# Attention and low-rank mixer: V in four row groups of the array, tails by a block-diagonal V, U into one group per head pair

## Chip, cores, metric

One core of one Trainium2 chip. The metric is the device time of a launch in microseconds (us), median of the runs.

## The reference, cut to what matters

Eight batches of causal attention with a decay bias (8 heads, 576 tokens, 64 per head), whose output x (576 x 512 per batch) goes through a low-rank mixing over tokens (rank 32) and a feed-forward:

```python
xt = x.transpose(0, 2, 1)                    # 512 x 576 per batch
h  = xt @ U @ V                              # U 576 x 32, V 32 x 576
u  = x + h.transpose(0, 2, 1)
out = u + np.maximum(u @ w_ch1, 0.0) @ w_ch2  # 512 -> 2048 -> 512
```

The change concerns `xt @ U @ V`. A "head pair" is 128 rows of xt; a batch has four.

## The kernel before

TensorE's order is written out by hand as tokens: SEQ for batches 0 and 1, PAIR for every later head pair. `U` is mix_in, `u` its copy out of PSUM, `Y` is mix_out (V), `y` adds x^T and writes u^T, `x` turns x by DMA, `F` is one step of feed-forward (four 512-column matmuls), `A`/`a` attention times v and its division, `D`/`E` scores, `G` the transposes of q and k on VectorE, `L` a step of the set-up of the decays, `p` a filler matmul (on the tile `warm`, its result unused). The other letters do not matter here.

```python
def mix_in(b):                       # U
    zp = z.rearrange("p (n c) -> p n c", n=PB)          # PB = 4 pairs
    for t in range(4):               # token block t into 32 PSUM rows, all four pairs at once
        nc.tensor.matmul(zp[ds(t * R, R)], lhsT=U_sb[:, t, :], rhs=x_of[b][:, :, t, :], start=True, stop=False, ...)
    for i in range(PB):              # the last 64 tokens of pair i
        nc.tensor.matmul(zp[ds(i * R, R), i, :], lhsT=U_sb[:, 4, :], rhs=x_of[b][:, i, 4, :], start=False, stop=True, ...)

def mix_out(n):                      # V, one pair; V_sb holds four stacked copies of V, so K = 128 sums the four partial products
    ...                              # cut: the 576 tokens in two pieces, two pairs share a bank `rest`
    if not mixed:                    # batches 0 and 1: x^T of the tail by an identity matmul
        nc.tensor.matmul(rest, lhsT=x_part(n, 4), rhs=identity[:, :64], start=True, stop=False, ...)
    for dst, lo, hi in pieces:
        nc.tensor.matmul(dst, lhsT=z_of[b][:, hp], rhs=V_sb[:, lo:hi], start=mixed, stop=True, ...)

xT = [stage[...] for i in range(3)]  # ring for x^T of batches 2 to 7
```

## Time and profile before

| | before |
|---|---|
| time, median of 4 runs | 370.0 us (369.4 to 370.3) |
| span of the profiled run | 367.9 us |
| TensorE, VectorE, ScalarE busy | 97%, 51%, 57% |
| U per batch, V per batch, in TensorE's stream | 0.48 us, 0.98 us |
| from one batch's U to the next, steady stage | 38.26 us |

The busy share says which engine is the bound; what an operation costs is read from the start times of matmuls, since each is still "busy" while the next already streams (a 512-column matmul is listed with 379 ns, the next one starts after 216). "Slot" below means this 0.216 us, and "stop" a gap beyond the slot. How to read the lines: in a timeline, start and duration in us, engine, line of the kernel, operation, tile written <- tiles read, shapes, count, and in brackets the idle time before with what ended it; in a list of waits, total us, times, longest. The lines follow inside the prediction.

### The profile page before, as it was taken

How to read it: one execution, taken by the hardware profiler on the slowest of the kernel's cores; microseconds unless marked ns; L12 is line 12 of the kernel's file. 1: busy time of each engine (PE TensorE's matmuls, PEld its weight loads, DVE VectorE, ACT ScalarE, POOL GpSimd, SP SyncE). 2: the span in 40 equal slices, each digit the busy share in tenths (PEclk: the TensorE clock that was granted, in tenths of full speed). 3: DMA queues.
4: the chain of work that ended last, by engine and by line, in shares of the span. 5: the costliest groups of instructions: out<-in, count | busy, mean ns of one | idle time of the engine just before them, and what ended most of it. 6: DMA issues, size and time to landing. Idle time of an engine off the chain costs nothing.

```text
span 367.9 us, 7782 instructions
## 1 busy us (share of the span) xinstructions
PE 355.9 (97%) x3036; PEld 197.1 (54%) x3036; DVE 187.5 (51%) x404; ACT 209.0 (57%) x407; POOL 108.6 (30%) x177
## 2 busy tenths in 40 slices
PE   8797999799999999999999999999999999999995
PEld 4576656356656655555555555555555444444443
DVE  7878756656658942864286536654453133011011
ACT  7697996248955686348734873388337602602600
POOL 8747461766435418040904080000000000000000
PEclk9999999999999999999999999999999999999999
DMA  7999999999999999995998899545115122113112
GB/s 95 165 185 124 143 152 205 169 241 188 154 152 174 186 155 149 157 161 109 150 136 144 148 114 119 152 114 77 51 64 98 37 76 85 30 43 99 31 41 74
DMA packets 112156, 45.53 MB, mean 124 GB/s; under 512 B 96448, under 2 KB 104000, under 8 KB 112120
## 3 DMA queue, kind: packets, MB, share of 16 engines
q0 software_dynamic: 65760, 18.54, 63.1%
q1 hardware_dynamic: 46360, 26.49, 36.9%
q8 instruction: 24, 0.39, 0.5%
q14 instruction: 12, 0.10, 0.1%
HBM read 37.73 MB, written 10.03 MB: 130 GB/s over the span
## 4 chain that ended last, share of the span: by engine, by line
PE 88%; DMA 5%; POOL 3%; DVE 2%; issue 1%; ACT 0%; POOLq 0%; ACTq 0%
PE pwork L477 34%; PE pwork L497 33%; PE pscore L265 10%; PE pwork L344 7%; DMA v_slot<-in_v_dram 3%; DMA U_sb<-in_moe_U_dram 2%; PE pwork L440 2%; POOL hT L120 1%; POOL v_slot L146 1%; PE pwork L375 1%; DVE turned L250 1%; DVE uT L463 0%; DVE x_sb L360 0%; DVE o_sb L510 0%; POOL stage L127 0%
## 5 line engine op out<-in xcount | busy, mean ns | idle before, releaser
L330 ACT ACTIVATE pT<-pscore 128x512 bf16<-128x512 f32 (+1 forms) x224 | 112.5, 568 | 69.6 <-PE pscore L265 67.2
L477 PE MATMUL pwork<-uT,w_sb 128*128 128x512 bf16 x576 | 134.1, 379 | 0.0
L497 PE MATMUL pwork<-w_sb,hT 128*128 128x512 bf16 (+2 forms) x592 | 132.0, 373 | 0.6 <-DVE o_sb L510 0.6
L484 ACT ACTIVATE hT<-pwork 128x512 bf16<-128x512 f32 x144 | 86.4, 618 | 53.9 <-PE pwork L477 53.3
L497 PEld LDWEIGHTS <-hT 128*128 128x128 bf16 x592 | 55.9, 98 | 60.2 <-issue 1.1
L477 PEld LDWEIGHTS <-w_sb 128*128 128x128 bf16 x576 | 53.9, 98 | 57.3 <-issue 1.5
L265 PE MATMUL pscore<-slot 128*128 128x128 bf16 (+4 forms) x576 | 61.9, 240 | 2.6 <-DVE slot L236 1.3
L250 DVE STREAM_TRANSPOSE turned<-qk_sd 128x576 bf16<-128x576 bf16 x48 | 54.2, 1130 | 7.6 <-DMA qk_sd<-in_q_dram 7.2
L510 DVE TENSOR_TENSOR o_sb<-pwork,stage 128x512 f32<-128x512 f32 (+2 forms) x37 | 24.8, 671 | 57.8 <-PE pwork L497 57.7
L265 PEld LDWEIGHTS <-slot 128*128 128x128 bf16 x576 | 39.7, 98 | 23.2 <-DVE slot L236 1.4
L359 DVE RECIPROCAL rec<-pwork 128x5 f32<-128x5 f32 x64 | 12.1, 188 | 77.0 <-PE pwork L344 76.7
L138 POOL DMA_DIRECT2D qk_sd<-in_q_dram x48 | 27.2, 578 | 77.6 <-DVE pT L333 38.3
L344 PEld LDWEIGHTS <-pT 128*128 128x128 bf16 x960 | 35.2, 98 | 7.1 <-issue 0.3
L344 PE MATMUL pwork<-v_slot,pT 128*128 128x65 bf16 x960 | 38.6, 194 | 0.2 <-DVE slot L236 0.2
L138 POOL DMA_DIRECT2D qk_sd<-in_k_dram x48 | 27.1, 575 | 22.2 <-DMA w_sb<-in_moe_w_ch_dram 15.5
L360 DVE TENSOR_TENSOR x_sb<-pwork,rec 128x320 bf16<-128x320 f32 x64 | 31.5, 492 | 2.2
L333 DVE TENSOR_TENSOR pT<-pT,keep 128x512 bf16<-128x512 bf16 (+1 forms) x84 | 28.1, 342 | 8.1 <-ACT pT L330 7.8
L146 POOL DMA_DIRECT2D v_slot<-in_v_dram x32 | 28.3, 907 | 3.5 <-DMA w_sb<-in_moe_w_ch_dram 2.4
L461 DVE TENSOR_TENSOR uT<-pwork,stage 128x384 bf16<-128x384 f32 (+7 forms) x48 | 19.1, 450 | 16.3 <-PE pwork L440 16.3
L236 DVE COPY slot<-pwork 64x576 bf16<-64x576 bf16 x21 | 16.7, 798 | 4.3 <-PE pwork L224 3.3
L557 PE MATMUL pwork<-warm 128*128 128x512 bf16 x38 | 10.7, 431 | 1.3 <-DVE warm L116 1.3
L440 PE MATMUL pwork<-V_sb,z_sb 128*128 128x512 bf16 (+6 forms) x64 | 11.7, 286 | 0.0
(76 smaller groups left out, 112.9 us busy)
## 6 DMA issues: line engine op xcount, KB each, us to landing
out_dram<-o_sb SPq DMA_DIRECT2D x35, 256.0 KB, 4.8
slot<-turned SPq DMA_DIRECT2D x96, 72.0 KB, 4.2
v_slot<-in_v_dram POOLq DMA_DIRECT2D x32, 128.0 KB, 7.3
w_sb<-in_moe_w_ch_dram POOLq DMA_DIRECT2D x8, 512.0 KB, 10.8
qk_sd<-in_q_dram POOLq DMA_DIRECT2D x48, 72.0 KB, 4.7
qk_sd<-in_k_dram POOLq DMA_DIRECT2D x48, 72.0 KB, 5.6
stage<-in_q_dram POOLq DMA_DIRECT2D x2, 288.0 KB, 9.4
stage<-in_k_dram POOLq DMA_DIRECT2D x2, 288.0 KB, 10.0
```

The source lines that it names most:

```text
L138: nc.gpsimd.dma_start(out=qk_t[g][ds(32 * a, 32), c, :].rearrange("p (n f) -> p n f", n=6), in_=src[g // 2, 4 * (g % 2) + a].rearrange("(n ...
L146: nc.gpsimd.dma_start(out=vt[:, t, :, 0:D], in_=v[b, :, ds(t * 128, 128), :].rearrange("h p d -> p h d"),)
L250: nc.vector.transpose(turned[:, e, c].rearrange("p (n m t) -> p n t m", n=6, t=3), src[:, c].rearrange("p (n t e d) -> p e n t d", n=6, t= ...
L265: nc.tensor.matmul(dst, lhsT=head_of(h)[:, ds(S + j * 128, 128)], rhs=head_of(h)[:, lo:hi], start=start, stop=stop and not bias, skip_grou ...
L330: nc.scalar.activation(dst, src, EXP, scale=scale)
L333: nc.vector.tensor_tensor(p, p, m, op=ALU.min)
L344: nc.tensor.matmul(po[:, i, :], lhsT=p_of(h)[:, ds(spot(j, i), 128)], rhs=v_slots[h // H % 3][:, j, h % H, :], start=(j == 0), stop=(j == ...
L360: nc.vector.tensor_tensor(x_of[b][:, h % H // 2, :, ts(h % 2, D)], po[:, :, 0:D], rec.to_broadcast([128, 5, D]), op=ALU.mult,)
L477: nc.tensor.matmul(f1, lhsT=w1_sb[nf // 4][:, kt, ds(nf % 4 * 128, 128)], rhs=uT[:, g % 4, kt, :], start=(kt == 0), stop=(kt == 3),)
L484: pending.append(lambda nf=nf, f1=f1: nc.scalar.activation(hT[:, nf, :], f1, RELU))
L497: nc.tensor.matmul(f2[:, lo:hi], lhsT=hT[:, nf, ds(i * 128, 128)], rhs=w2_sb[nf // 4][:, nf % 4, lo:hi], start=(nf == 0), stop=nf == NF - ...
L510: nc.vector.tensor_tensor(o_sb[:, lo:hi].rearrange("p (d c) -> p d c", c=128), f2[:, lo:hi].rearrange("p (d c) -> p d c", c=128), u_sb[g % ...
```

## The change

Intent: V has only 32 rows, so four pairs can use four 32-row strips of the array at once. For that U must leave pair i's product in partitions 32i to 32i+31, and four PSUM banks must be open together. The tails (64 tokens) of all pairs come from one matmul with a block-diagonal V. The whole token order, the order of loads and the bank list were redone around it, and x^T got a fourth buffer because all four pairs of a batch are now alive together.

```diff
 def mix_in(b):
-        for t in range(4): ... four 512-column, then four 128-column matmuls
+        for t in range(5):
+            for i in range(PB):
+                nc.tensor.matmul(
+                    z[ds(i * R, R), 0:128],
+                    lhsT=U_sb[:, t, :],
+                    rhs=x_of[b][:, i, t, :],
+                    start=(t == 0), stop=(t == 4), ...)
 def mix_keep(copy, b):
-        copy(z.rearrange("p n c -> p (n c)"), z_of[b])      # 512 columns
+        copy(z, z_of[b][:, 0:128])
-    def mix_out(n): ...
+    def mix_out(b):
+        for i, n in enumerate(pairs):
+            nc.tensor.matmul(
+                mix_of[n],                                  # four banks
+                lhsT=z_of[b][ds(i * R, R), :],
+                rhs=V_sb[ds(i * R, R), 0:512],
+                start=mixed, stop=True, ...)
+        rest = pwork()
+        ...                                                 # batches 0, 1: x^T tails, as before
+        nc.tensor.matmul(rest[:, 0 : PB * 64], lhsT=z_of[b], rhs=V_sb[:, 512:], start=mixed, stop=True, ...)
+        # V_sb[:, 512:] is built by four small copies on VectorE (token Z2)
-    "k0 s0 v0 s1 w1 u1 u0 w0 v1 w3 w2 q4 x0 x1 x2 x3 q5 v2 "      # loads: u = U, V; w, x = the two weights
+    "k0 s0 v0 s1 u0 w0 u1 w2 w1 v1 w3 q4 x0 x1 x2 x3 q5 v2 "
-    PAIR: ... U-1@1 uA-1@1 ... Y-5@1 Y-4@1 ... Y-4@2 ... Y-3@2 ...
+    PAIR: ... U-1@1 F yA-3@2 uV-1@1 x-3@3 d1 f1 f0 Y-1@1 a-1 K0 yV-5@1 ...
     (SEQ, PAIR and the bank list are new throughout; fillers 38 -> 43; ring of x^T 3 -> 4)
```

## The prediction

> **What bounds the kernel now.** I read the page first: engine shares, then the chain that ended last, then the busy time by stage, then the waits of TensorE, and last the timeline around the two operations that the change touches (L375/L384 multiply by U, L440 by V). From the page:
>
> ```profile
> PE 355.9 (97%) x3036; PEld 197.1 (54%) x3036; DVE 187.5 (51%) x404; ACT 209.0 (57%) x407; POOL 108.6 (30%) x177
> ...
> PE 88%; DMA 5%; POOL 3%; DVE 2%; issue 1%; ACT 0%; POOLq 0%; ACTq 0%
> ```
>
> TensorE is the bound, and 88% of the last chain is its own work. Busy is not the same as streaming, so the stages (stretch, sum, then PE, PEld, DVE, ACT, POOL busy):
>
> ```profile
> 9.90:24.00 14.10, 12.34 (x126) 8.17 (x127) 10.82 (x18) 10.37 (x21) 7.73 (x11) 1.00 1.76 173
> 24.00:37.50 13.50, 11.19 (x224) 9.20 (x223) 11.32 (x26) 11.08 (x23) 9.43 (x15) 1.00 1.32 143
> 37.50:67.40 29.90, 28.00 (x303) 17.02 (x301) 20.76 (x47) 23.07 (x48) 12.06 (x21) 1.00 1.28 169
> 67.40:123.00 55.60, 55.60 (x506) 31.74 (x505) 36.47 (x75) 34.84 (x75) 32.66 (x51) 1.00 1.82 177
> ```
>
> From 67.4 us on TensorE never rests, until the last microseconds: a nanosecond taken from its stream there is a nanosecond off the end. Before 37.5 us it has gaps, and part of its work is filler (38 matmuls on the tile warm, some 8 us); VectorE and ScalarE are each busy about 80% and pass work to one another. Work taken from TensorE there is worth little; what counts is when the first feed-forward matmul (L477) can start. TensorE's waits are few:
>
> ```profile
> PE pwork L427 <- DVE uT L463: 2.8, 2, 1.9
> ...
> PE pwork L375 <- DMA U_sb<-in_moe_U_dram: 0.9, 1, 0.9
> ```
>
> The first is two stops while a shared PSUM bank for the last 64 tokens is emptied, in batches 0 and 1. The second looks like a late load of U, and the new order of loads moves U forward. But VectorE's timeline (first line) and TensorE's (second) say otherwise:
>
> ```profile
> 32.18 0.49 DVE L360 TENSOR_TENSOR x_sb<-pwork,rec 128x320 bf16<-128x320 f32 x1
> ...
> 32.83 0.40 PE L375 MATMUL pwork<-x_sb,U_sb 128*32 128x512 bf16 x4 [0.95 <-DMA U_sb<-in_moe_U_dram]
> ```
>
> The last normalised attention tile, which U multiplies, is finished at 32.67 us, 0.16 us before. Loading U earlier gains next to nothing by itself.
>
> **What the Trainium skill says.** (1) "TensorE: Matmul & The Clock Gate", Part 1, gives start to start N / 2.4 GHz + about 2.5 ns when warm, 215.7 ns for N = 512. The trace agrees: four L477 matmuls take 0.86 us on the chain, 0.216 each. (2) The same page, Part 3, says matmuls in different row or column groups run together, one duration plus about 4 ns per further tile, and that four row groups at K = 32, N = 512 measured 3.07 times. The trace before has column groups only, and for them agrees: four at L375 take 0.40 us together where one takes 0.39. Row groups no run here shows yet. (3) "TensorEngine Tiling (Array Packing)", Key Properties: changing the tiling mode drains the array. The timeline shows the price:
>
> ```profile
> 138.76 1.03 PE L477 MATMUL pwork<-uT,w_sb 128*128 128x512 bf16 x4
> ...
> 139.72 0.40 PE L375 MATMUL pwork<-x_sb,U_sb 128*32 128x512 bf16 x4
> 139.73 0.11 PEld L384 LDWEIGHTS <-U_sb 128*32 128x32 bf16 x4
> 139.94 0.23 PE L384 MATMUL pwork<-x_sb,U_sb 128*32 128x128 bf16 x4
> ...
> 140.10 0.61 PE L477 MATMUL pwork<-uT,w_sb 128*128 128x512 bf16 x2
> ```
>
> The slots of the four L477 end at 138.76 + 4 x 0.216 = 139.62. U starts at 139.72, so 0.09-0.10 is lost going in; its first four take 0.22, the next four 0.06; L477 is back at 140.10, so 0.10 is lost coming out. U costs 0.48 us per batch. (4) The tiling page, Gotcha 1: row groups must write to different PSUM banks. The new code gives each head pair its own bank, so V now needs five banks at one moment.
>
> **V, the main gain.** Before, a batch b >= 2 multiplies each of four pairs by all 576 columns of V:
>
> ```profile
> 144.97 0.65 PE L440 MATMUL pwork<-V_sb,z_sb 128*128 128x320 bf16 x4
> ...
> 145.46 1.03 PE L497 MATMUL pwork<-w_sb,hT 128*128 128x512 bf16 x4
> ```
>
> Two pairs hold the stream from 144.97 to 145.46, 0.49 us; a batch 0.98. After: 0.10 in, four concurrent 512-column matmuls 0.216 + 3 x 0.004 = 0.23, 0.10 out, then one 256-column matmul on the block-diagonal V, 256 / 2.4 + 2.5 = 0.11: 0.54 us. Saved 0.44 per batch. Batches 0 and 1 also add x^T by an identity; that stays, and V itself shrinks by the same 0.44. Eight batches: **-3.5 us**. I take -3.3, because four weight loads of 128 columns into row groups may not hide as well as the 32-column loads at L384 do.
>
> **U.** Before: four of 512 and four of 128 columns, 0.48. After: five rounds of four 128-column matmuls, 5 x (0.056 + up to 0.012) = 0.28-0.34, plus 0.20 for the changes of mode: 0.48-0.54. **+0.2 us** over eight batches. Its copy out of PSUM shrinks from 512 to 128 columns (0.585 to about 0.28 us, the duration of the 128-column exponential), off the bound, but it shortens the way from U to V.
>
> **Batch 1.** The timeline there:
>
> ```profile
> 64.66 0.41 PE L440 MATMUL pwork<-V_sb,z_sb 128*128 128x512 bf16 x2
> 66.96 0.19 PE L427 MATMUL pwork<-identity,x_sb 128*128 128x64 bf16 x1 [1.90 <-DVE uT L463]
> ```
>
> One bank per batch for the tails, written once, ends this wait: **-1.9 us**, undiluted since TensorE is otherwise full here. In the new order the wait that could replace it is V on the copy of z. Between them stand four L477 matmuls (0.86) and an x^T (0.22); the copy needs some 0.2 after U, 0.3 itself, and at most one ReLU (0.62) ahead of it. It fits.
>
> **Opening.** The chain in order of time:
>
> ```profile
> 12.41 11.38 DMA v_slot<-in_v_dram
> 24.66 8.13 DMA U_sb<-in_moe_U_dram
> 37.71 0.87 PE pwork L477 x4
> ```
>
> The first batch's v lands near 23.8 us, and its loads stand as early in the new order as in the old. So attention times v cannot start sooner, even though the new token order has three more exponentials done by then. From there VectorE has eight divisions (0.68 each), three copies of q/k (0.80), a set-up of decays (0.6) and the four small copies of V's tail (0.5): about 9 us, so U starts near 33.5, somewhat later than now (32.83). After it the new order is shorter: no stop at L427 (0.9), V at once, smaller copies. I expect the first L477 group to end near 37.6 instead of 38.4, and one transpose and one score tile (0.5) have moved ahead of it: **-1.2 us**. The five extra filler matmuls (1.1 us) fall into idle time.
>
> **New waits.** In the steady stage V asks for four pair banks and one tail bank, and they are freed one by one by VectorE's additions (about 0.95 us per pair). In the instruction listing with the banks filled in, V follows U by 0.97 us, and VectorE has to finish a 1.13 us transpose and the copy of z in between; some 0.4 us are left over. The tightest reuse comes after batch 2's V: the second pair's bank is wanted 3.1 us later, about when VectorE gets there. I add **+0.5 us** for all such stops.
>
> Sum: -3.3 + 0.2 - 1.2 - 1.9 + 0.5 = -5.7 us, and 370.0 - 5.7 = **364.3 us** (-1.5%).
>
> **Rivals.** A: row groups do not overlap (they share the write port to PSUM, or the loads serialise). Then V costs 4 x 0.216 + 0.11 + 0.20 = 1.17 per batch, 0.19 more than now, and the result is about 369. For it: no row group in this trace. Against: column groups overlap as the page says. B: the five banks at once turn into stops of half a microsecond in each of six batches, +3, some 367. For it: TensorE has not one wait between 67.4 us and the last tile, so any new one shows in full; against: VectorE is busy only 57-66% there. C: the opening is bound more softly than I think, ScalarE runs through earlier, and Q/K copies and exponentials gain 3 us instead of 1.2; then 362, just past 2%. For it: the order of all tokens was redone and ScalarE idles over 3 us before 16.2 us; against: v's landing.
>
> **Range and chances.** The V saving is sure to some 0.5 us if row groups overlap; opening and new waits may each be off by 1.5 us. Together 361.8 to 366.8. Beyond 2% means under 362.6, which needs C and no new waits: 0.23. Slower by 2% would need stalls of 13 us: 0.02.
>
> **What would show it.** Right: four 512-column matmuls at V starting within 15 ns of one another, V with its modes about 0.54 us per batch; no wait of TensorE on VectorE's copies near 65 us; U still starting at about 33; the stream after 67 us without waits over 0.3 us. Wrong: V's four starting 0.2 us apart (A), waits for VectorE's additions or the copy of z in every batch (B), first L477 well before 36 us (C), or first L477 later than now.

## The result, and the profile after

The changed kernel took 364.47 us (363.95 to 366.81, 4 runs) against 370.0 (369.43 to 370.32), ratio 0.9865, 95% interval 0.9819 to 0.9910. A ratio here is the mean time of one kernel's runs over that of the other's of the same rounds, so not quite the ratio of the medians. 364.3 was predicted; "within 2%" was right.

The page after:

```profile
PE 354.9 (98%) x3113; PEld 195.6 (54%) x3113; DVE 192.1 (53%) x437; ACT 204.0 (56%) x402; POOL 109.3 (30%) x178
...
PE 81%; DMA 14%; POOL 3%; issue 1%; DVE 0%; POOLq 0%
```

TensorE is busy for only 1.0 us less although the span lost 4.8: the other 3.8 were idle time, and busy time counts the overlap of neighbours. The second line is the news: of the chain of work that ended last, DMA has gone from 5% to 14%. The stages after, columns as before (stretch, sum, then PE, PEld, DVE, ACT, POOL):

```profile
24.00:37.50 13.50, 12.40 (x231) 9.85 (x230) 11.74 (x31) 10.81 (x24) 8.81 (x13) 1.00 1.28 162
37.50:67.40 29.90, 29.21 (x299) 17.03 (x298) 19.41 (x42) 21.82 (x47) 13.87 (x23) 1.00 1.58 171
67.40:123.00 55.60, 55.60 (x535) 31.91 (x534) 39.75 (x84) 35.41 (x79) 32.27 (x52) 1.00 1.87 174
```

The steady stage is as full as before, so no new stop came in there. TensorE's timeline in it, around U (L376) and V (L415, tails L434):

```profile
143.51 0.60 PE L266 MATMUL pscore<-slot 128*128 128x448 bf16 x4
144.04 0.46 PE L376 MATMUL pwork<-x_sb,U_sb 128*32 128x128 bf16 x20
144.44 1.04 PE L492 MATMUL pwork<-w_sb,hT 128*128 128x512 bf16 x4
145.41 0.39 PE L415 MATMUL pwork<-V_sb,z_sb 32*128 32x512 bf16 x4
145.73 0.28 PE L434 MATMUL pwork<-V_sb,z_sb 128*128 128x256 bf16 x1
145.85 1.46 PE L492 MATMUL pwork<-w_sb,hT 128*128 128x512 bf16 x6
```

The four L492 slots from 144.44 (the first some 0.01 longer) end at 145.31; V is over at 145.85: **0.54 us**, against 0.98 before. Of it 0.10 goes to entering the row groups, 0.23 to all four matmuls (they start 3 to 4 ns apart in the trace), 0.10 to leaving, 0.11 to the tails. U's five rounds start 56 to 65 ns apart and U costs 0.49. From one batch's U to the next it is now 37.83 us, 0.43 less than before.

Before the steady stage TensorE's waits are others than in the kernel before; from the list of waits of the changed kernel:

```profile
PE pscore L266 <- DVE slot L237: 1.2, 1, 1.2
...
PE pwork L492 <- DMA w_sb<-in_moe_w_ch_dram: 0.6, 1, 0.6
PE pscore L266 <- DVE x_sb L361: 0.4, 1, 0.4
```

The stops at the shared tail bank (2.8 us before) are gone, and a wait for the second weight is new. It stands in the timeline just ahead of U of batch 1:

```profile
63.07 0.63 PE L345 MATMUL pwork<-v_slot,pT 128*128 128x65 bf16 x15
64.27 1.89 PE L492 MATMUL pwork<-w_sb,hT 128*128 128x512 bf16 x8 [0.58 <-DMA w_sb<-in_moe_w_ch_dram]
66.09 0.46 PE L376 MATMUL pwork<-x_sb,U_sb 128*32 128x128 bf16 x20
```

Where the time came from, by the starts of matmuls in the two profiled runs:

| stretch | before | after | change |
|---|---|---|---|
| to the first L472 (the first feed-forward matmul; L477 before) of batch 0 | 37.55 | 37.44 | -0.1, with one transpose and one score tile more done (0.5) |
| from there to that of the second group | 42.56 | 40.81 | -1.75 |
| from there to the last matmul | 284.25 | 281.66 | -2.6 (6 x 0.43) |

Together -4.4 us; the profiled times differ by 4.7, and the last 0.3 of it lies behind the last matmul. The first row holds for this pair only: in two more profiled runs of the same changed kernel (e0 and e9 below) the first L472 starts at 39.2 and 39.3 us, 1.7 us later than in the kernel before, which was profiled once.

Sorted by cause over the whole stream of this pair: V's matmuls -5.1 us; changes of tiling mode +1.5 to +1.8 and stops of TensorE -2.2 to -2.6 (from about 10 to 7.6; some gaps are both); U +0.1; fillers +1.1; and +0.3 because more of the first fillers (nine and a part of a tenth, not eight) start 0.42 us apart and not 0.216.

### The profile page after: what moved, and what is told of

Same layout as the page of the kernel before. It is cut to its first block, busy times and chain, and to the rows that moved or that the text cites. A ratio compares the mean times of both kernels' runs of the same rounds, so it can differ in the third digit from the quotient of the medians.

```text
span 363.1 us, 7898 instructions
## 1 busy us (share of the span) xinstructions
PE 354.9 (98%) x3113; PEld 195.6 (54%) x3113; DVE 192.1 (53%) x437; ACT 204.0 (56%) x402; POOL 109.3 (30%) x178
## 4 chain that ended last, share of the span: by engine, by line
PE 81%; DMA 14%; POOL 3%; issue 1%; DVE 0%; POOLq 0%
PE pwork L492 34%; PE pwork L472 30%; PE pscore L266 9%; PE pwork L345 6%; DMA w_sb<-in_moe_w_ch_dram 4%; DMA U_sb<-in_moe_U_dram 3%; DMA v_slot<-in_v_dram 3%; DMA stage<-in_k_dram 2%; DMA qk_sd<-in_q_dram 2%; POOL hT L121 1%; PE pwork L376 1%; PE pwork L415 1%; PE pwork L434 0%; DVE o_sb L505 0%; POOL v_slot L147 0%
## 5 line engine op out<-in xcount | busy, mean ns | idle before, releaser
L331 ACT ACTIVATE pT<-pscore 128x512 bf16<-128x512 f32 (+1 forms) x224 | 110.8, 558 | 60.8 <-PE pscore L266 58.6
L492 PE MATMUL pwork<-w_sb,hT 128*128 128x512 bf16 (+2 forms) x592 | 133.6, 373 | 1.2 <-DVE o_sb L505 0.6
L472 PE MATMUL pwork<-uT,w_sb 128*128 128x512 bf16 x576 | 133.6, 379 | 0.1
L479 ACT ACTIVATE hT<-pwork 128x512 bf16<-128x512 f32 x144 | 83.8, 610 | 68.6 <-PE pwork L472 67.9
L492 PEld LDWEIGHTS <-hT 128*128 128x128 bf16 x592 | 54.8, 98 | 58.9 <-issue 1.4
L472 PEld LDWEIGHTS <-w_sb 128*128 128x128 bf16 x576 | 53.9, 98 | 57.2 <-issue 0.3
L266 PE MATMUL pscore<-slot 128*128 128x128 bf16 (+3 forms) x576 | 66.5, 240 | 1.8 <-DVE slot L237 1.2
L266 PEld LDWEIGHTS <-slot 128*128 128x128 bf16 x576 | 42.2, 98 | 28.1 <-DVE slot L237 1.3
L334 DVE TENSOR_TENSOR pT<-pT,keep 128x512 bf16<-128x512 bf16 (+1 forms) x84 | 25.5, 350 | 0.7 <-ACT pT L331 0.7
L237 DVE COPY slot<-pwork 64x576 bf16<-64x576 bf16 x24 | 18.5, 794 | 0.5 <-ACT slot L237 0.2
L456 DVE TENSOR_TENSOR uT<-pwork,stage 128x64 bf16<-128x64 f32 (+6 forms) x54 | 15.3, 349 | 2.0 <-PE pwork L415 1.9
L552 PE MATMUL pwork<-warm 128*128 128x512 bf16 x43 | 12.6, 435 | 1.3 <-DVE warm L117 1.3
L237 ACT COPY slot<-pwork 64x576 bf16<-64x576 bf16 x8 | 6.4, 801 | 2.8 <-DVE slot L237 2.6
```

Of the source, the lines that this page charges most:

```text
L237: copy(dst[:, :, :, :, par], tp_of[h][par * D : par * D + D].rearrange("p c t m -> p c m t"),)
L266: nc.tensor.matmul(dst, lhsT=head_of(h)[:, ds(S + j * 128, 128)], rhs=head_of(h)[:, lo:hi], start=start, stop=stop and not bias, skip_grou ...
L331: nc.scalar.activation(dst, src, EXP, scale=scale)
L334: nc.vector.tensor_tensor(p, p, m, op=ALU.min)
L472: nc.tensor.matmul(f1, lhsT=w1_sb[nf // 4][:, kt, ds(nf % 4 * 128, 128)], rhs=uT[:, g % 4, kt, :], start=(kt == 0), stop=(kt == 3),)
L479: pending.append(lambda nf=nf, f1=f1: nc.scalar.activation(hT[:, nf, :], f1, RELU))
```

## Experiments

Twelve runs of kernels (e0 to e3; e5 to e8; e4 and e9 to e11), each on one chip with runs of the kernel before between. Kernels are compared by their ratios to it (R), and through the profiled runs.

**e0, e9: the changed kernel again** (twice, as base).

> The changed kernel again, on the chip of the experiments, as their base. If the first measurement is sound, its fast runs lie at 0.985 to 0.989 of the kernel before (364 to 366 us).

> The changed kernel once more as the base of this chip: 0.984 to 0.987 of the kernel before. The runs so far suggest that its spread of 364 to 366.8 us is the end of the last second-weight transfer (62 to 65.5 us) plus a constant; the profiled run should obey time = that landing + 0.6 + 300.6 us, or 364.0 if it lands before 63 us.

e0: 365.43 us (364.43 to 366.53), before 371.3, R 0.9841 (0.9808 to 0.9875). e9: 364.26 (363.62 to 365.52), before 369.89, R 0.9849 (0.9824 to 0.9874). With the first measurement: the gain is 1.4 to 1.6%, and the changed kernel varies by 3 us from run to run. The rule written for e9 failed: the weight landed at 62.7 us (its last packet), and still the profiled run took 365.52, not 364.0. The table at the end of this section says what set it.

**e1: V's four row groups issued twice in batches 2 to 7.**

```diff
-        for i, n in enumerate(pairs):
+        for i, n in enumerate([*pairs] * (2 if mixed else 1)):
+            i %= PB
```

> The four concurrent 512-column matmuls of V are issued twice for the six batches from 2 on (the second set overwrites, the result stays right). Theory: a set of four takes 0.23 us of the stream, so +6 x 0.23 = +1.4 us over the changed kernel. Rival (row groups overlap only in part, and the saving came from elsewhere): a set of four takes up to 0.86 us, +5.2 us.

366.18 us, R 0.9861 (e0 0.9841: +0.7 us, within their intervals no clear difference). The trace is sharper than the times. Its timeline:

```profile
145.37 0.61 PE L416 MATMUL pwork<-V_sb,z_sb 32*128 32x512 bf16 x8
145.91 0.28 PE L435 MATMUL pwork<-V_sb,z_sb 128*128 128x256 bf16 x1
```

From V's start to the tails it is 0.54 us where the changed kernel has 0.32: four more matmuls of 512 columns cost **0.22 us**, the stream time of one. From U to U it is 38.05 us against 37.83, and from U of batch 1 to the end of the run 300.1 us against 298.8: +1.4, as the theory said. The rival, partial overlap, is out.

**e2: the row groups alone undone.** V as four full-array matmuls on a block-diagonal V, everything else as changed but for a larger memset on GpSimd at the start.

```diff
-                lhsT=z_of[b][ds(i * R, R), :],
-                rhs=V_sb[ds(i * R, R), 0:512],
+                lhsT=z_of[b],
+                rhs=V_full[:, i, :],          # 128 x 4 x 512, zero but for V in rows 32i..32i+31
```

> The row groups alone undone: the same order, banks and ring, but V as four full-array 512-column matmuls on a block diagonal V, no change of tiling mode. Theory: per batch 4 x 0.216 + 0.11 = 0.97 against the 0.54 us read from the trace of the changed kernel, +0.43 each, +3.4 us in all (some 0.2 less where a batch of the first two has it beside a wait). Rival (the new token order gives the gain, the row groups little): +1 us or less.

368.3 us, R 0.9925 (0.9882 to 0.9969) against 0.9841 (0.9808 to 0.9875) for e0: +3.1 us, clear of the noise. The timeline:

```profile
146.12 1.03 PE L416 MATMUL pwork<-V_full,z_sb 128*128 128x512 bf16 x4
146.98 0.27 PE L435 MATMUL pwork<-V_sb,z_sb 128*128 128x256 bf16 x1
147.09 1.24 PE L493 MATMUL pwork<-w_sb,hT 128*128 128x512 bf16 x5
```

V takes 146.12 to 147.09, 0.97 us, and the period is 38.26, the one of the kernel before to the hundredth. So the row groups bring 0.43 us a batch, over half of the whole gain; the new order, banks and block diagonal without them bring the rest (R 0.9925), and all of that lies before the steady stage (from the first feed-forward matmul of the second group to the last matmul e2 has 284.24 us, the kernel before 284.25).

**e3: the loads in the old order.**

```diff
-        "k0 s0 v0 s1 u0 w0 u1 w2 w1 v1 w3 q4 x0 x1 x2 x3 q5 v2 "
+        "k0 s0 v0 s1 w1 u1 u0 w0 v1 w3 w2 q4 x0 x1 x2 x3 q5 v2 "
```

> The changed kernel with the loads in the order of the kernel before (U behind one block of the first weight and V, the second weight block first). Theory of the prediction: U needs the last normalised tile anyway, which comes after 33 us, so at most 0.3 us either way. Rival (the load of U had held up the opening): U starts later and the kernel takes 0.5 to 1 us longer.

364.97 us, R 0.9843 against 0.9841: no difference, so in the changed kernel the order of the loads costs nothing that shows. It says less about the kernel before: in e3's profiled run U's two loads had landed by 32.4 us, and U started at 35.15 because the x tiles came later. In the kernel before, U's first load landed 0.12 us after the last x tile, and its second piece, the last 64 rows, only at 33.23. One line further in its timeline the matmuls on that piece stand:

```profile
33.36 0.24 PE L384 MATMUL pwork<-x_sb,U_sb 128*32 128x128 bf16 x4
```

They start 0.53 us after L375's 32.83, where the steady stage has 0.22. So U's load did hold U there, by 0.16 us and then 0.3; what that was worth at the end of the run was not tested.

**e4: the ring of x^T back to three.**

```diff
-            out=xT[n % 4], ...        turned = xT[n % 4] ...
+            out=xT[n % 3], ...        turned = xT[n % 3] ...
```

> The ring of x^T back to three buffers, all else as changed. The transpose of a batch's last pair then waits for the additions of its first pair, which in the new order come some 8 us later in the same iteration, and SyncE[...] holds back the transfers behind it. Theory: TensorE then waits for q/k slots or for a drained output bank in each batch, 1 to 6 us in all. Rival: the transfers behind have that much slack, no change within 0.3 us, and the ring of four is not needed.

372.07 us, R 1.008 (8.5 us over e9, more than the 1 to 6 expected), and a wrong result: the token order issues the transpose of a batch's fourth pair ahead of the additions of its first, so with three buffers the first pair's x^T is overwritten. I had taken it that the transfer would wait for the additions; it is the other way round. A line of VectorE's waits and the first of TensorE's:

```profile
DVE uT L456 <- DMA stage<-x_sb: 12.4, 4, 4.2
```

```profile
PE pwork L492 <- DVE uT L456: 3.8, 4, 2.7
```

The additions wait for a transfer of x^T, and TensorE for the banks that they free. With this token order the fourth buffer is not a refinement but part of doing all four pairs at once. What a correct order with three buffers would cost stays open.

**e5: sixteen fillers fewer.**

```diff
-  ... d1 p4 D3 ... p2 p2 p2 R2 ... D4 p3 f3 ... E6 p2 A4 ... l4 p1 tA13 ...
+  ... d1 D3 ... R2 ... D4 f3 ... E6 A4 ... l4 tA13 ...
```

> The changed kernel without 16 of its 43 filler matmuls (those after the first 27; 3.5 us of stream, all before the first feed-forward matmul). Theory: they stand in idle time, so within 0.4 us of the changed kernel (ratio to the kernel before 0.983 to 0.985), the waits of TensorE in the opening grow by some 3 us instead. Rival 1: they delay real work, then 0.5 to 3 us faster. Rival 2: they keep the granted clock up, then slower and a granted clock under 1 in the trace.

364.9 us, R 0.9849, the same as e9, within what was expected (0.983 to 0.985) and with no difference to show; granted clock 1.0 in the profiled run. TensorE's listed waits ahead of the first L472 grew from 3.3 us to 5.4, as the theory has it. The fillers stand in idle time, to within half a microsecond.

**e6, e7, e8: a lighter VectorE in the opening, the last second-weight block out of the way, both.** In the changed kernel VectorE's opening contains, ahead of U (the first block of lines is VectorE's, the second TensorE's):

```profile
28.89 1.01 DVE L565 CAST V_sb<-V_tail 32x64 bf16<-32x64 f32 x4
...
33.66 0.49 DVE L361 TENSOR_TENSOR x_sb<-pwork,rec 128x320 bf16<-128x320 f32 x1
```

```profile
34.10 0.56 PE L376 MATMUL pwork<-x_sb,U_sb 128*32 128x128 bf16 x20
```

U starts as soon as VectorE has made the last x tile, so e6 takes work from VectorE; e7 takes away the transfer that TensorE waits for at 64 us.

```diff
 e6, e8: the four V-tail copies on nc.scalar instead of nc.vector, token Z2 after d7; first decay step L from before U0 to behind D10
 e7, e8: "... x0 x1 x2 x3 q5 v2 " -> "... x0 x1 x2 q5 v2 ",  rhs=w2_sb[min(nf // 4, 2)]   (wrong result on purpose)
```

> The changed kernel with VectorE's opening lightened: the four small copies of the tail of V (1.0 us in the trace) go to ScalarE, which idles there for 2 us, and the set-up of the second half of the decays (0.7 us) goes behind the first V. Theory: U of batch 0 and the first feed-forward matmul move forward by about 1 us, but the last block of the second weight, whose transfer ends near 64 us, makes TensorE wait that much longer (1.5 us instead of 0.6), and the time stays within 0.3 us. Rival: nothing behind it holds, and the time falls by 1 us.

> Wrong result on purpose: the last block of the second weight is not loaded, its matmuls read the block before it. Theory: the wait for that transfer at 64 us goes (0.6 to 1.2 us in the traces so far), and the time falls by 0.7 us, to a ratio of about 0.982. Rival: another wait takes its place at once, no change.

> Both at once, wrong result on purpose. Theory: now the microsecond won in the opening comes through, -1.7 us against the changed kernel (ratio about 0.9795), 1 us below the one without the last weight block alone. Rival: the same as that one, and the lighter opening is worth nothing even with the transfer out of the way.

e6: 365.83 us, R 0.9877. e7: 364.51, R 0.985. e8: 364.18, R 0.9854, five of its six runs between 364.11 and 364.20. None differs clearly from the changed kernel (0.9841 to 0.9865, on other chips). For e6 the rival (1 us faster) falls, but my theory is not shown by it either: TensorE has two stops of 0.9 us together (near 40 and 42 us), which I put down to the place of the moved decay step, and only 0.2 us of stop at the weight. Its profiled run, 364.14, was also the fastest of its six. For e7 the wait did go, but the gain of 0.7 did not show in the time. e8's microsecond did not come through.

**e10, e11: a version meant to keep.** e10 puts the first quarter of the second output tile ahead of the last quarter of the first, in the first output group, so that the last weight block is wanted 0.86 us later. e11 is that, with the V-tail copies on ScalarE and the decay steps in VectorE's long wait for the third batch's q.

```diff
 e10 (narrow, g == 0): order of quarters (tile, quarter):  ... (0,2) (0,3) (1,0) (1,1) ...
                                                       ->  ... (0,2) (1,0) (0,3) (1,1) ...
 e11: e10 + V-tail copies on nc.scalar after d7, tokens "L L" directly before the first G4
```

> The changed kernel with one exchange in the first output group: the first quarter of its second tile goes ahead of the last quarter of its first tile, so that the last second-weight block is needed 0.86 us later; result right. Theory: the wait at 64 us (0.6 to 1.3 us) shrinks to under 0.3, time down by 0.5 to 0.7 us against the changed kernel, with less spread. Rival: another wait (for the bank of the second tile, or for the last attention tile) takes its place, no change.

> The same exchange, and VectorE lightened in the opening with the decays' set-up moved into VectorE's 6 us wait for the third batch's q (where the lighter version before had put it among slot copies, and made TensorE wait 0.9 us). Theory: the first feed-forward matmul starts 0.5 to 1 us earlier; the transfers (q of the third batch at 49 us, the last second-weight block at 63 to 65) do not, so at most 0.3 us of that reaches the end. Rival: all of it reaches the end, 1 us below the exchange alone.

e10: 364.5 us (363.95 to 364.74), R 0.9847 against e9's 0.9849: no gain, though the stop at the weight is down to 0.08 us. e11: 363.87 us (363.15 to 364.52), R 0.9832 (0.9807 to 0.9856): the lowest of all, clearly below the kernel before, but not separated from the changed kernel. Its two waits that matter (VectorE's, then TensorE's):

```profile
DVE turned L251 <- DMA qk_sd<-in_q_dram: 5.5, 1, 5.5
```

```profile
64.80 1.02 PE L494 MATMUL pwork<-w_sb,hT 128*128 128x512 bf16 x4 [0.16 <-DMA w_sb<-in_moe_w_ch_dram]
```

**What the profiled runs say together.** From U of batch 1 on, these kernels are one and the same machine: the time of the profiled run is that U's start plus 298.8 us (298.76 to 298.86 in the ten rows). So the table holds all that varies in them:

| run | first L472 | U of batch 1 | between | TensorE's stop for v / for the last weight block | time |
|---|---|---|---|---|---|
| changed | 37.44 | 66.09 | 28.65 | - / 0.58 | 364.85 |
| e0, changed | 39.20 | 67.77 | 28.57 | 1.6 / 0.94 | 366.53 |
| e9, changed | 39.29 | 66.76 | 27.47 | 1.5 / - | 365.52 |
| e3, old loads | 38.49 | 67.32 | 28.83 | 1.2 / 1.2 | 366.11 |
| e5, fewer fillers | 36.90 | 66.29 | 29.39 | - / 1.3 | 365.15 |
| e6, light VectorE | 36.90 | 65.33 | 28.43 | - / - | 364.14 |
| e7, no last block | 38.15 | 65.63 | 27.48 | 0.9 / - | 364.41 |
| e8, both | 37.21 | 65.43 | 28.22 | - / - | 364.20 |
| e10, exchange | 37.17 | 65.44 | 28.27 | - / - | 364.29 |
| e11, exchange and light | 36.92 | 65.75 | 28.83 | - / 0.16 | 364.52 |

A first L472 before 37.5 never gave a U of batch 1 before 65.3. The stretch between takes 27.5 us when TensorE is late and has almost no stop there (e7, e9; e1 and e2 as well), and 28.2 to 29.4 otherwise. The trace shows what lies in the rest: stops at the last weight block (changed, e0, e3, e5), and stops of 0.5 to 1.1 us in all near 53 us among the scores (changed, e5, e10, e11), which come after VectorE's wait of 5.5 to 6.4 us for the third batch's q (changed, e10, e11; that this wait makes them is argued, not tested). In e6 and e8 it is the two stops near 40 us (0.9 us). And the start itself depends on the first v: the same changed kernel, e0 and then e9, at its first attention times v:

```profile
25.60 0.84 PE L345 MATMUL pwork<-v_slot,pT 128*128 128x65 bf16 x21 [1.57 <-DMA v_slot<-in_v_dram]
```

```profile
25.00 0.31 PE L345 MATMUL pwork<-v_slot,pT 128*128 128x65 bf16 x5 [0.98 <-DMA v_slot<-in_v_dram]
```

So in the profiled runs the first 66 us are paced largely by transfers (v near 24, q of the third batch near 49, the second weight near 64), which land earlier or later from run to run; e9 has a late v alone, e0 a late v and then a late weight. That the three share one cause, the loaded DMA queues, is argued, not shown. A second source of spread stays open: the slowest run of the changed kernel (366.81 us) and that of e8 (367.32) show a granted clock of 0.994, where the profiled runs lie at 0.998 to 1.0. Neither was profiled.

## Why the prediction was right

It named 364.3 us; 15 runs of the changed kernel average 365.0, the first four have the median 364.5. The mechanism of the main term was right; the smaller terms were off in both directions, and that the sum still lay near is partly luck. Step by step:

- **V, -3.3 us: right.** V's matmuls -5.1 and mode changes +1.5 to +1.8 over the stream make -3.3 to -3.6. A batch went from 0.98 to 0.54 us, as summed; e1 and e2 confirm the overlap and its size by themselves. The allowance for weight loads that hide badly was not needed.
- **U, +0.2: right in size, +0.1.** 0.48 became 0.49.
- **No stop in the steady stage** beyond what was summed: right, and better than the +0.5 allowed. VectorE's 0.4 us of room between U and V was enough in all six batches. Rivals A (no overlap) and B (bank stalls) are out.
- **U's load is not what holds U:** half right. In the changed kernel the last x tile holds U. In the kernel before the load cost 0.16 us, as said, and another 0.3 at its second piece (33.36 in its timeline), which was overlooked.
- **Batch 1, -1.9: mis-sized.** The stop at the shared bank is gone, but the next matmuls there want the last block of the second weight. Already in the kernel before, its last packet came at 65.4 us and its landing was signalled at 66.2; the output group reached that block at 67.24, so without the 1.9 us stop it would have been there at 65.3, some 0.9 us before the data. The stop hid a later one. In the profiled pair all stops of TensorE between the first two L472 groups fell only from 2.2 to 1.4 us: -0.8, where -1.9 had been summed. The prediction had looked for the wait that could replace it in the copy of z, not in the transfers. (Its "it fits" there is 0.04 us short by its own numbers, 0.2 + 0.3 + 0.62 = 1.12 against 0.86 + 0.22 = 1.08; no ReLU stood ahead of the copy, and V did not wait.)
- **Opening, -1.2: half at best.** In the profiled pair the first L472 came 0.1 us earlier, with 0.5 us of work moved ahead of it; in e0 and e9 it came 1.7 us later than in the kernel before, which the prediction had named as a sign of being wrong ("first L477 later than now"). The sum also counts batch 0's V (0.4) twice, among the eight batches and here as "V at once". U started at 34.1 and not 33.5, because the V-tail copies took 1.0 us and not 0.5. e6 and e8, which take this work from VectorE, did not win the microsecond back: in their profiled runs TensorE is stopped again before 66 us.
- **Rival C (3 us in the opening) is out:** no profiled run has the first L472 before 36.9 us. v's landing, the reason given, is seen as a stop in e0, e3, e7 and e9.

The profiled pair alone gives 4.7 us (369.58 to 364.85), nearer than the sum of 5.7 to a change that is V's row groups (3.2 with U) plus 1.5 of rest; the medians give 5.5. What makes up the difference between the pair and the medians was not tested; the spread from run to run is as large.

## What to carry to other kernels

With K = 32, four row groups cost here the stream of one matmul plus two changes of tiling mode, 0.43 us against 0.86: worth it when four wide matmuls can be brought together, and the producers, PSUM banks and buffers that must be alive together for it are part of the price. Before adding up the waits that a change removes, look for what stands right behind each: here, behind a stop of two microseconds, a weight transfer that would have come a microsecond too late. Where a steady stage repeats, read the change from its period; it showed 0.22 us a batch (e1) where the times, which move by 3 us from run to run, could not separate 0.7 us.

## What the Trainium skill lacked or had wrong

- "TensorEngine Tiling (Array Packing)", Key Properties, says that a change of tiling mode drains the array, without a figure. Here it is 0.09 to 0.10 us going in and as much coming out, for column groups (U) and row groups (V) alike; with both, four 512-column row groups hold the stream for 0.43 us, half of 4 x 0.216.
- "TensorE: Matmul & The Clock Gate", Part 3, gives 3.07 times for four row groups at K = 32, N = 512, without saying whether the changes of mode are in it. Inside the mode, e1 shows 0.22 us for four more against 0.86, 3.9 times; with both changes it is the 2 times above.
- The same page, Part 1, says that start to start never drops below about 25 ns. Between groups of one round it is 2 to 4 ns here, as its Part 3 has it; rounds of U on the same column groups start 56 ns apart (the first two 65), as Part 1 gives for N = 128.
- None of the pages drawn on here tells how far the landing of one and the same load moves between runs: the last second-weight packet came between 62.7 and 65.5 us in three profiled runs of the changed kernel.
